# A spectral filter beside product-key experts: first transform by pairs of tiles, forward stage in four-byte 32x32 blocks, and a new order

## The chip, the cores and the metric

One core of a Trainium2 chip runs the whole program. The time is device microseconds of that core, from a run's first instruction to its last with what lies around them. Lower is better.

## The reference

`x` has 2048 rows of 576. It is normalised by rows, and two branches of the normalised `xn` are added to it.

```python
xn = _layernorm(x, axis=-1)
return x + _A_ref(xn, A_w_r, A_w_i) + _B_ref(xn, B_w_q, B_k1, B_k2, B_u, B_v)

# A: a filter in the frequency plane
X = rfft2(xn, axes=(-2, -1)) * (w_r + 1j * w_i)
y = irfft2(X, s=(S, D))

# B: for each of 32 heads the best of 8 + 8 keys picks one of 64 experts
q = einsum("nd,dhc->nhc", xn, w_q);  q1, q2 = q[..., :128], q[..., 128:]
i1, i2 = argmax(q1 @ k1.T), argmax(q2 @ k2.T);  e = i1 * 8 + i2
out = sum over heads of gelu(xn @ u[e]) * v[e]          # softmax over one entry is 1
```

## The kernel before

The 2048 rows lie as 16 tiles `t` of 128 rows (row 16 n + t is in partition n). `XN` holds all of `x`.

**Spectral branch.** The transform over the 2048 rows is split as 128 times 16. `folds(t)` uses the symmetry of cosine and sine: it adds and subtracts a tile's columns and their mirror image (`t1` buffers, then `A2` buffers), so that later transforms run over 145 and 144 columns. `dft128(t)` multiplies the folded tile by the 128-point matrix `Rs` (four-byte matmuls; `Rs` is the constant `Rm` times the row scale `rr`), and its result is split into two two-byte halves, `AB` (128 partitions) and `ABL` (the 33 columns left over). Row frequencies now lie in 16 groups `g`. `d_fwd(g)` transforms along the 576 columns (`c16` holds its two-byte constants, forward and inverse) and splits its result into two halves again: ScalarE copies it as the high half, VectorE subtracts for the low one. `s_fwd(g)` does the 16-point stage for groups g and g+1: 64x64 blocks with constants `s16`, three matmuls for each product (high by high, low by high, high by low). `s_mul(g)` multiplies by the filter `W`, scaled by its largest element (`w_scale`), `s_inv(g)` and `d_inv(t)` go back, and `fin(t)` does the inverse 128-point stage with `RT`, adds the experts' part and `x`, and stores.

**Expert branch.** Only differences of keys matter, so `fold_part(b, s)` multiplies `w_q` by them: 16 calls, each with two loads `w` of 576 KB and eight matmuls against `KP` (four-byte; four blocks of 128x32 side by side). `fold_scale`, `fold_end` and `fold_last` bring the result into `MU` and `MUL`. Then `x_t(r)` loads and scales the transposed `x`, `scores(r)` multiplies it by `MU`, and `route(r)` and `combine(r)` pick the experts and build `CAT` for `fin`. All scores wait for the last `fold_part`.

**Order.** Calls are not issued as written. `_Plan.add` records each operation; matmuls in a row of one stage are joined up to a planned cost of 900. `issue` then emits all operations in the order of a table of numbers, `RANK`; a string `PICK` says for the free choices which engine does it (`v` VectorE, `a` ScalarE, `g` GpSimd). `follow` walks the same order to place PSUM tiles in the eight banks. Each engine runs its instructions in that order. All loads and stores are issued by SyncE, whose queue is in order too: a load that waits for its buffer holds up those behind it. Every instruction is emitted in one line, L493, so the profile's rows are told apart by tiles: `banks` is PSUM, `A` an `A2` buffer, `s` the `s16` constants, `c` a constant (`c32` or `c16`), `t` a `t1` or `t2` buffer.

Of the kernel before, what the change touches and what calls it, by code (L numbers as in the profile page):

```python
# [32 lines left out]
def _consts():  # L33
# [40 lines left out]
    pair = np.arange(128).reshape(16, 2, 2, 2).transpose(2, 0, 1, 3).ravel()  # L74
    row = np.arange(128).reshape(16, 2, 2, 2).transpose(1, 0, 2, 3).ravel()
# [3 lines left out]
    def halves(m):  # L79
        return np.concatenate([m[:, :64, :64], m[:, 64:, 64:]], 1)  # L80

    def tr(m):
        m = m.transpose(0, 2, 1).reshape(16, 128, 16, 8).transpose(0, 1, 3, 2).reshape(16, 128, 128)
        return halves(m)
# [3 lines left out]
    U, V = halves(U[:, row]), halves(V[:, row])  # L88
    fw = np.concatenate([U, V, -U], 2)
    swap = np.arange(128) ^ 64  # L90
    kk[1::2], iv[1::2] = kk[1::2][:, swap], iv[1::2][:, swap]
    s16 = np.concatenate(_hl(fw * 64) + _hl(iv), 2)
# [7 lines left out]
    C1 = np.where((j <= 144)[:, None] == ev[None, :], C1, 0)  # L100
    S1 = np.sin(pi2 * (d1[:, None] * ll[None, :] % 576) / 576)
# [27 lines left out]
    c16 = np.concatenate([dc.reshape(128, -1), dl.reshape(128, -1),  # L129
                          ic.reshape(128, -1), il.reshape(128, -1)], 1)  # L130
    return c32, c16, s16, kk, ll


INF = float("inf")

# [1054 lines left out]
```

## Time and profile before

| | |
|---|---|
| median of 3 runs | 214.52 us (214.12 to 215.97) |
| the profiled execution | 214.62 us, span 212.8 us |
| TensorE clock granted | 0.998 |
| read from HBM, written | 38.33 MB, 4.72 MB |
| PE, DVE, POOL, ACT busy | 192.7, 195.5, 136.1, 129.8 us |

PE is TensorE, PEld its weight loads, DVE VectorE, ACT ScalarE, POOL GpSimd, SP SyncE. A row of the groups reads: line, engine, operation, output<-inputs, shape, count, then busy us and mean ns of one, then the idle time just before and who ended it. PE's busy time is modelled from pipelined matmuls; what a matmul costs is read from one start to the next.

### The profile page before, as it was taken

The page shows a single profiled execution, that of the slowest core. Times are in us where ns is not written, and L with a number is a line of the kernel's source. Part 1 is how long each engine was busy: PE and PEld are TensorE (multiplying, and loading weights), DVE is VectorE, ACT ScalarE, POOL GpSimd, SP SyncE. Part 2 cuts the span into 40 slices and gives each one's busy share as a digit, 9 for nine tenths or more (in the row PEclk, how much of TensorE's full clock was granted, in tenths as well). Part 3 has the DMA queues.
Part 4 walks back from the last instruction along what each step waited for, and adds up shares of the span by engine and source line. Part 5 has one row for each costly group of instructions (what it writes and reads, how often), then busy time and mean ns, then how long its engine had stood idle before and what let it go on. Part 6 is the DMA issues. An engine that isn't in the chain of part 4 may idle for free.

```text
span 212.8 us, 5984 instructions
## 1 busy us (share of the span) xinstructions
PE 192.7 (91%) x2287; PEld 134.7 (63%) x2287; DVE 195.5 (92%) x471; ACT 129.8 (61%) x280; POOL 136.1 (64%) x199
## 2 busy tenths in 40 slices
PE   0069998989998999999999999999999999999992
PEld 0067765677765775847465656665566887687871
DVE  0999999898799999997999999999999999999972
ACT  2278988788756973896958554757676453122430
POOL 2777789673339822885498244966696379549870
PEclk9999999999999999999999999999999999999999
DMA  5999999999999999308436012451100001071156
GB/s 159 398 414 425 408 401 395 370 366 403 372 313 353 391 269 373 102 34 338 147 104 223 10 40 64 137 184 32 38 0 5 0 5 55 0 273 63 55 204 243
DMA packets 14572, 43.43 MB, mean 204 GB/s; under 512 B 1872, under 2 KB 4688, under 8 KB 14160
## 3 DMA queue, kind: packets, MB, share of 16 engines
q1 hardware_dynamic: 14544, 43.05, 55.3%
q8 instruction: 18, 0.29, 0.6%
q14 instruction: 10, 0.08, 0.1%
HBM read 38.33 MB, written 4.72 MB: 202 GB/s over the span
## 4 chain that ended last, share of the span: by engine, by line
PE 44%; DVE 30%; DMA 8%; POOL 8%; issue 6%; ACT 1%; SPq 0%; POOLq 0%; DVEq 0%
PE banks L493 44%; DVE t L493 7%; DMA w<-in_wq_dram 6%; DVE w L493 5%; DVE A L493 5%; POOL A L493 4%; DVE MT L493 4%; DVE AB L493 3%; DMA XN<-in_x_dram 3%; POOL t L493 2%; DVE mx L493 2%; DVE st L493 2%; DVE XN L493 1%; DVE ABL L493 1%; POOL mv L493 1%
## 5 line engine op out<-in xcount | busy, mean ns | idle before, releaser
L493 PE MATMUL banks<-MU,xT 128*128 128x512 f16 x192 | 46.1, 380 | 0.0
L493 POOL TENSOR_TENSOR A<-t 128x287 f32<-128x287 f32 (+3 forms) x46 | 31.4, 698 | 10.5 <-DVE t L493 5.7
L493 PEld LDWEIGHTS <-xT 128*128 128x128 f16 x224 | 21.0, 98 | 22.7 <-DVE MU L493 0.2
L493 PE MATMUL banks<-c,AB 128*128 128x145 f16 (+1 forms) x384 | 34.4, 228 | 0.0
L493 PEld LDWEIGHTS <-AB 128*128 128x128 f16 x384 | 31.5, 122 | 1.7
L493 PE MATMUL banks<-Rs,A 128*128 128x128 f32 x128 | 19.8, 302 | 13.9 <-DVE Rs L493 12.6
L493 POOL TENSOR_TENSOR xT<-xf,xT 128x512 f16<-128x512 f32 (+1 forms) x28 | 24.1, 863 | 11.9 <-PE banks L493 5.5
L493 POOL TENSOR_TENSOR y<-t,t 128x289 f32<-128x289 f32 x30 | 20.8, 713 | 16.7 <-DVE t L493 16.1
L493 PEld LDWEIGHTS banks<-Rs,A 128*128 128x128 f32 x128 | 17.3, 209 | 17.2 <-DVE Rs L493 13.1
L493 POOL TENSOR_TENSOR yh<-y,yh 128x578 f16<-128x578 f32 x16 | 20.9, 1311 | 8.0 <-ACT yh L493 5.9
L493 DVE SCALAR_TENSOR_TENSOR t<-banks,wx,Wt 128x578 f32<-128x578 f32 x32 | 24.2, 812 | 0.4 <-PE banks L493 0.3
L493 PE MATMUL banks<-A,c 128*128 128x288 f32 x64 | 21.9, 424 | 0.4 <-DVE XN L493 0.4
L493 DVE TENSOR_TENSOR AB<-banks,AB 128x512 f16<-128x512 f32 x32 | 21.5, 676 | 0.3 <-ACT AB L493 0.3
L493 PE MATMUL banks<-w,KP 128*32 128x288 f32 x256 | 20.3, 415 | 1.1 <-DMA w<-in_wq_dram 0.9
L493 ACT ACTIVATE yh<-banks,sc 128x580 f32<-128x580 f32 x16 | 11.5, 744 | 15.8 <-PE banks L493 11.5
L493 ACT ACTIVATE AB<-banks 128x512 f16<-128x512 f32 x32 | 18.7, 591 | 3.1 <-PE banks L493 2.9
L493 PE MATMUL banks<-c,ABL 99*128 99x289 f16 (+1 forms) x64 | 18.5, 290 | 0.0
L493 ACT ACTIVATE ABL<-banks 99x256 f16<-99x256 f32 x32 | 12.0, 381 | 8.4 <-PE banks L493 7.8
L493 POOL TENSOR_TENSOR t<-yh 128x288 f32<-128x288 f32 x16 | 12.2, 765 | 6.6 <-ACT yh L493 4.1
L493 ACT ACTIVATE MT<-banks 128x256 f16<-128x256 f16 (+1 forms) x12 | 5.7, 472 | 16.5 <-PE banks L493 14.7
L493 POOL TENSOR_TENSOR t<-XN 128x289 f32<-128x289 f32 x17 | 13.1, 776 | 3.0 <-DMA XN<-in_x_dram 2.2
L493 DVE SCALAR_TENSOR_TENSOR XN<-banks,sc,XN 128x576 f32<-128x576 f32 (+1 forms) x18 | 13.1, 743 | 1.5 <-PE banks L493 1.4
(136 smaller groups left out, 438.2 us busy)
## 6 DMA issues: line engine op xcount, KB each, us to landing
w<-in_wq_dram SPq DMA_DIRECT2D x32, 576.0 KB, 6.8
xf<-in_xT_dram SPq DMA_DIRECT2D x16, 320.0 KB, 3.4
Wt<-in_W_dram SPq DMA_DIRECT2D x8, 578.0 KB, 5.1
out_dram<-XN SPq DMA_DIRECT2D x14, 288.0 KB, 3.2
XN<-in_x_dram SPq DMA_DIRECT2D x3, 1154.0 KB, 9.6
s<-in_s_dram SPq DMA_DIRECT2D x16, 192.0 KB, 4.1
XN<-in_x_dram SPq DMA_DIRECT2D x2, 577.0 KB, 5.0
c<-in_c_dram SPq DMA_DIRECT2D x1, 868.5 KB, 7.2
```

Source lines behind the costliest of these rows:

```text
L493: fn(*[x.place() if isinstance(x, _Ps) else x for x in args], **{k: x.place() if isinstance(x, _Ps) else x for k, x in kw.items()})
```

## The change

- **First transform.** `folds(t, n)` takes two tiles at once (the first two tiles are loaded, normalised and folded singly); `dft128(t)` takes a pair and three banks, and its evictions are twice as wide. The row mean is no longer subtracted: the column of the zero frequency is zero in the forward constants.
- **Forward stage.** `d_fwd` leaves its result in four bytes, one copy and no subtraction. `s_fwd(g, m)` does four groups and one of the two output parts, in 32x32 blocks of four bytes: 32 matmuls into four tiles of one bank. `s_mul(g, m)` multiplies one part by both parts of the filter; the splitting into halves moves to `s_inv`.
- **Constants.** `s16` becomes `fw` (four-byte, one load for four groups) and `iv` (two-byte, one load for two groups); `c16` becomes `cf` (forward) and `ci` (inverse), two loads.
- **Filter scale** for four groups at once, then four times; before one of four groups and six of two.
- **End.** `d_inv` takes two tiles; the factor `sc[12]` is multiplied into `RT` once.
- **Order, engines and buffers**: `RANK` and `PICK` are new; some buffers have another count (`xf` 2 for 3, `A2` 6 for 4).

```diff
+    def quarters(m):
+        return np.concatenate([m[:, 32 * a:32 * a + 32, 32 * a:32 * a + 32] for a in range(4)], 1)
...
+    C1[:, ll == 0] = 0
...
 RANK = (
-    3, 19, 14, 16, 76, 107, 2, 75, 51, 39, 143, 181, 0, 6, 15, 22, 13, 25, 1, 12, 40, 237, 5, 4, 8, 9, 7,
+    3, 9, 4, 8, 10, 11, 13, 2, 58, 18, 59, 67, 516, 5, 17, 7, 16, 15, 182, 25, 0, 1, 6, 20, 19, 34, 36, 23,
...
-    LOADS = ((0, 2), (2, 2), (4, 4), (8, 4), (12, 4))
+    LOADS = ((0, 1), (1, 1), (2, 2), (4, 4), (8, 4), (12, 4))
...
-    def folds(t):
-        xn = XN[:, t]
-        e = T([128, 2, L], F32, "eo", 2, "t1")
-        FG.tt(e[:, 1], xn[:, 0:289], xn[:, 576:287:-1], OP.subtract)
-        FG.tt(e[:, 0], xn[:, 0:289], xn[:, 576:287:-1], OP.add)
...
-        V.scalar_tensor_tensor(F[:, 0, 0:145], e[:, 0, 0:145], rr[:, 2, t:t + 1], e[:, 0, 288:143:-1],
-                               op0=OP.add, op1=OP.add)
+    def folds(t, n):
+        x = XN[:, t:t + n]
+        e = T([128, n, 2, L], F32, "eo", 4, "t1")
+        FV.tt(e[:, :, 0], x[:, :, 0:289], x[:, :, 576:287:-1], OP.add)
+        FG.tt(e[:, :, 1], x[:, :, 0:289], x[:, :, 576:287:-1], OP.subtract)
+        F = T([128, n, 2, L], F32, "F", 6, "A2")
+        FV.tt(F[:, :, :, 0:145], e[:, :, :, 0:145], e[:, :, :, 288:143:-1], OP.add)
+        FV.tt(F[:, :, :, 145:289], e[:, :, :, 143::-1], e[:, :, :, 145:289], OP.subtract)
...
+        p = PS("x", (128, 3, 512))
...
     def d_fwd(g):
...
-        t = T([128, 2, 2, L], F16, "A2", 2)
-        FP.copy(t[:, 0], p[:, :, :L])
-        V.tensor_tensor(t[:, 1], p[:, :, :L], t[:, 0], op=OP.subtract)
-        A2[g] = t
+        A2[g] = T([128, 2, L], F32, "A2", 6)
+        FP.copy(A2[g], p[:, :, :L])
...
-    def s_fwd(g):
-        ps = [PS("b"), PS("b")]
...
-                            P.matmul(ps[q][o:o + 64, m, :L], s[r, ha, 64 * w:64 * w + 64], A2[g + q][r, hb, b, :],
-                                     start=(n == 0), stop=(n == 5), tile_position=(64 * e, o))
+    def s_fwd(g, m):
+        ps = [PS("q", (128, 512)) for q in range(4)]
+        plan.pack, plan.cap = {p.tile for p in ps}, 1400
+        for b in range(2):
+            w = 32 * (0, 1, 1, 2)[2 * m + b]
+            for k in range(4):
+                r = slice(32 * k, 32 * k + 32)
+                for q in range(4):
+                    o = 32 * (k ^ q)
+                    P.matmul(ps[q][o:o + 32, :L], FW[g][r, q, w:w + 32], A2[g + q][r, b, :], start=(b == 0), stop=(b == 1),
+                             tile_position=(32 * k, o))
...
-    def s_mul(g):
+    def s_mul(g, m):
+        x, w, sw = PF.pop(g)[:, :L].unsqueeze(1).to_broadcast([128, 2, L]), Wt[g], wx[:, 1, g:g + 1]
+        if m == 0:
+            Y[g] = T([128, 2, L], F32, "y", 4)
+            V.scalar_tensor_tensor(Y[g], x, sw, w, op0=OP.mult, op1=OP.mult)
+            return
+        y, t = Y[g], T([128, 2, L], F32, "t1", 4)
+        V.scalar_tensor_tensor(t, x, sw, w, op0=OP.mult, op1=OP.mult)
+        FG.tt(y[:, 0], y[:, 0], t[:, 1], OP.subtract)
+        FG.tt(y[:, 1], y[:, 1], t[:, 0], OP.add)
...
-    for g in range(4):
-        load_s16(g)
+    load_fw(0)
     w_scale(0, 4)
...
+    for g in range(0, 16, 4):
+        for q in range(g, g + 4):
+            d_fwd(q)
+            if q % 2 == 0:
+                if q > 2:
+                    load_w(q)
+                load_iv(q)
...
+        for m in range(2):
+            s_fwd(g, m)
+            for q in range(4):
+                s_mul(g + q, m)
```

What the new order and the new loads do is shown at three places. The first is SyncE's queue in the middle of the `wq` loads (`w`): `c_72` is the whole `c16`, `s_0` and its like one group's `s16`, `xf` transposed `x`. Before:

```order
L493 DMA w_118<-in_wq_dram 128x1152
L493 DMA c_72<-in_c_dram 128x3474
L493 DMA xf_123<-in_xT_dram 128x640
L493 DMA Wt_113<-in_v_dram 128x576
L493 DMA w_119<-in_wq_dram 128x1152
L493 DMA s_0_114<-in_s_dram 128x768
L493 DMA w_120<-in_wq_dram 128x1152
L493 DMA s_1_115<-in_s_dram 128x768
L493 DMA w_122<-in_wq_dram 128x1152
```

and in the change, where buffers of one name are one tile (`cf`, `fw` and `iv` are the new constants):

```order
L491 DMA w<-in_wq_dram 128x1152 x2
L491 DMA cf<-in_cf_dram 128x1734
L491 DMA w<-in_wq_dram 128x1152 x2
L491 DMA xf<-in_xT_dram 128x640
L491 DMA w<-in_wq_dram 128x1152 x3
L491 DMA fw<-in_fw_dram 128x384
L491 DMA w<-in_wq_dram 128x1152 x2
L491 DMA iv<-in_iv_dram 128x768
```

`c16` is loaded by half, and one `fw` and one `iv` stand where `s16` loads for four groups began. The second place is the same queue at the last `wq` loads. Before, with the filter (`Wt`) for the fourth pair of groups behind:

```order
L493 DMA w_121<-in_wq_dram 128x1152
L493 DMA s_1_115<-in_s_dram 128x768
L493 DMA s_0_114<-in_s_dram 128x768
L493 DMA w_118<-in_wq_dram 128x1152
L493 DMA w_119<-in_wq_dram 128x1152
L493 DMA w_122<-in_wq_dram 128x1152
L493 DMA s_2_116<-in_s_dram 128x768
L493 DMA s_3_117<-in_s_dram 128x768
L493 DMA Wt_112<-in_W_dram 128x1156
```

and in the change:

```order
L491 DMA w<-in_wq_dram 128x1152 x5
L491 DMA Wt<-in_W_dram 128x1156
L491 DMA w<-in_wq_dram 128x1152 x3
L491 DMA Wt<-in_W_dram 128x1156
L491 DMA xf<-in_xT_dram 128x640
L491 DMA iv<-in_iv_dram 128x768
L491 DMA fw<-in_fw_dram 128x384
```

No constants stand among the last eight `wq` loads any more, but one filter load, for groups 4 and 5, does; `iv` and `fw` for later groups and `ci` (after these rows) come behind. The third place is PE where the first forward stage follows a fold. Before, weight loads and matmuls of two groups alternate:

```order
L493 LDWEIGHTS AB
L493 MATMUL banks<-c_72,AB 128x145
L493 MATMUL banks<-w_120,KP 32x288 x4
L493 LDWEIGHTS s_0_114
L493 MATMUL banks<-A_0_98,s_0_114 64x289
L493 LDWEIGHTS s_1_115
L493 MATMUL banks<-A_1_99,s_1_115 64x289
```

and in the change:

```order
L491 MATMUL banks<-w,KP 32x288 x8
L491 MATMUL banks<-A_95,fw 32x289 x32
L491 LDWEIGHTS ABL
L491 MATMUL banks<-cf,ABL 128x289
L491 LDWEIGHTS AB
```

Four-byte matmuls carry their weight loads with them, so the half stage is one row of 32, and `d_fwd` of a later group follows it; the second half stands behind `d_fwd` and two more fold groups. In all there are 64 matmuls of the forward stage, 126 of `d_fwd` and 66 of `s_inv` ahead of the last fold group in the change, against 144, 112 and 144 before.

More of the change, by code (lines that the diff above doesn't have):

```diff
@@ L390, in add @@
         if (eng == "tensor" and last is not None and last.eng == eng and last.stage == self.stage
-                and last.cost + c < 900 and (last.tiles == tiles or last.tiles | tiles <= self.pack)):
+                and last.cost + c < self.cap and (last.tiles == tiles or last.tiles | tiles <= self.pack)):
             op, i = last, len(self.ops) - 1
@@ new lines, in dft128 @@
+        p = PS("x", (128, 3, 512))
+        for i in range(2):
+            for c in range(4):
+                b, s = divmod(c, 2)
+                P.matmul(p[:, i, 128 * c:128 * c + 128], F[i][:, b, 161 * s:161 * s + 128], Rs[i], start=True, stop=True)
+        for i in range(2):
+            for b in range(2):
+                P.matmul(p[:99, 2, 256 * i + 128 * b:256 * i + 128 * b + 128], FL[i][:, b].rearrange("p a b -> p (a b)"),
+                         Rs[i], start=True, stop=True)
+        n = slice(2 * t, 2 * t + 4)
@@ L709, in dft128 @@
+        m = p[:, 0:2].rearrange("p i (h e) -> p h i e", e=2)
+        hi, ab = (AB[:, q].rearrange("p c (h n) -> p (c h) n", n=32)[:, :, n].rearrange("p h (i e) -> p h i e", e=2)
+                  for q in range(2))
         FP.copy(hi, m)
         V.tensor_tensor(ab, m, hi, op=OP.subtract)
-        lo = ABL[:99].rearrange("p b (h n) -> p (b h) n", n=64)[:, :, 4 * t:4 * t + 4]
+        l = p[:99, 2].rearrange("p (i h e) -> p h i e", i=2, e=2)
+        lo = ABL[:99].rearrange("p b (h n) -> p (b h) n", n=32)[:, :, n].rearrange("p h (i e) -> p h i e", e=2)
@@ new lines, in s_fwd @@
+    def s_fwd(g, m):
+        ps = [PS("q", (128, 512)) for q in range(4)]
+        plan.pack, plan.cap = {p.tile for p in ps}, 1400
+        for b in range(2):
+            w = 32 * (0, 1, 1, 2)[2 * m + b]
[5 more added lines that the diff above has]
+                             tile_position=(32 * k, o))
+        plan.pack, plan.cap = set(), 900
+        for q in range(4):
@@ L1003, in s_mul, with s_inv @@
+    @staged
+    def s_inv(g):
+        y = Y.pop(g)
         yh = T([128, 2, 2, L], F16, "yh", 2)
@@ L1076, in fin @@
             Q.dma_start(os[:, t, 288 * a:288 * b], x[:, 288 * a:288 * b])
-    for k, (t, n) in enumerate(LOADS):
+    for t, n in LOADS:
+        for i in range(t, t + n, 2):
+            folds(i, min(2, n))
         ln(t, n)
-        for i in range(t, t + n):
-            folds(i)
-            if i:
-                dft128(i - 1)
-    dft128(15)
+        for i in range(t & ~1, t + n & ~1, 2):
+            dft128(i)
     x_scale()
@@ L1114, in _body @@
     fold_last()
-    for r in range(3):
+    for r in range(2):
         x_t(r)
-    scores(0)
-    for g in range(4):
-        d_fwd(g)
-    s_fwd(0)
-    s_mul(0)
-    s_mul(1)
-    s_fwd(2)
-    for g in range(16):
-        s_inv(g)
-        if g + 2 < 16:
-            s_mul(g + 2)
-        if g + 4 < 16:
-            d_fwd(g + 4)
-            load_s16(g + 4)
-            if g % 2 == 1:
-                s_fwd(g + 3)
-        if g + 4 < 16 and g % 2 == 1:
-            load_w(g + 3)
-            w_scale(g + 3, 2)
-        r = g // 2
-        if g % 2 == 0:
-            if r < 5:
-                x_t(r + 3)
+    for g in range(0, 16, 4):
[5 more added lines that the diff above has]
+                load_iv(q)
+        if g:
+            w_scale(g, 4)
+        if g:
+            load_fw(g)
+        for m in range(2):
+            s_fwd(g, m)
+            for q in range(4):
+                s_mul(g + q, m)
+        for q in (g, g + 2):
+            s_inv(q)
+            s_inv(q + 1)
+            r = q // 2
+            scores(r)
+            if r < 6:
+                x_t(r + 2)
             route(r)
-        else:
-            if r < 7:
-                scores(r + 1)
             combine(r)
     w_end()
-    yq = {0: d_inv(0)}
-    for t in range(16):
-        if t + 1 < 16:
-            yq[t + 1] = d_inv(t + 1)
-        fin(t, yq.pop(t))
+    Q.dma_start(ci, a["ci"])
+    y = d_inv(0)
+    for t in range(0, 16, 2):
+        n = d_inv(t + 2) if t < 14 else None
+        for q in range(2):
+            fin(t + q, y[:, q])
+        y = n
 def _arrays(inp):
-    c32, c16, s16, kk, ll = _consts()
+    c32, cf, ci, fw, iv, kk, ll = _consts()
     g = lambda n: np.asarray(inp[n])
@@ L1173, in _arrays @@
         "c32": c32,
-        "c16": c16,
-        "s16": s16,
+        "cf": cf,
+        "ci": ci,
+        "fw": fw,
+        "iv": iv,
     }
```

253 lines of the change are left out of this document (111 added, 142 removed), and 123 rows, old and new, of the table RANK.

## Prediction

> **What bounds the kernel now.** I read the page's parts 1 and 2 first, then a table of busy time by stage, then the chain of waits.
>
> ```profile
> span 212.8 us, 5984 instructions
> ...
> PE 192.7 (91%) x2287; PEld 134.7 (63%) x2287; DVE 195.5 (92%) x471; ACT 129.8 (61%) x280; POOL 136.1 (64%) x199
> ...
> DMA  5999999999999999308436012451100001071156
> ```
>
> PE and DVE are both above 90%, and the DMA line reads nine tenths from 5 us to about 85 us and little afterwards. So the span has two parts with different limits. The table by stage (us of the stage, then busy us of each engine with its count, granted clock, DMA share, GB/s):
>
> ```profile
> core 0: us, PE busy (x) PEld busy (x) DVE busy (x) ACT busy (x) POOL busy (x), PEclk, DMA share, GB/s
> 12.60:50.00 37.40, 35.32 (x311) 26.98 (x312) 35.54 (x109) 31.45 (x87) 28.29 (x45) 1.00 1.01 396
> 50.00:84.00 34.00, 32.91 (x579) 23.23 (x578) 31.41 (x71) 23.48 (x48) 16.28 (x22) 1.00 0.99 355
> 84.00:130.00 46.00, 46.00 (x537) 28.15 (x537) 43.92 (x95) 32.84 (x61) 30.03 (x36) 1.00 0.37 123
> 130.00:170.00 40.00, 39.89 (x564) 26.07 (x553) 39.75 (x92) 26.18 (x57) 26.68 (x34) 1.00 0.19 59
> 170.00:209.00 39.00, 38.56 (x313) 30.23 (x311) 37.31 (x81) 12.20 (x22) 28.25 (x42) 1.00 0.28 105
> ```
>
> From 84 us on PE is busy 124.5 of 125 us, at full clock, while the DMA engines are at a third of their time. Before 84 us the DMA share is 1.0, and PE has lost 3.2 us of 71.4 since its first matmul. What ties the two parts together is the chain:
>
> ```profile
> 76.56 0.17 SPq L493
> 76.78 6.19 DMA w<-in_wq_dram
> 83.02 47.76 PE banks L493 x566
> ...
> 185.07 23.89 PE banks L493 x183
> 208.98 0.52 DVE XN L493
> ```
>
> The last load of `wq` lands at 83.0, the last fold matmuls follow (sixteen passes, about 1 us by the rows below), and then PE runs with hardly a gap to 185.07 + 23.89 = 209.0. So the span is made of three terms: the end of the last fold, **T**, at about 84.0; what PE has left after it, **R** = 209.0 - 84.0 = 125.0; and a tail of 212.8 - 209.0 = 3.8. The profiled execution took 214.62 us, so 1.8 us lie around the span; the median of the runs shown is 214.52.
>
> **T, the loads.** The two halves of the loaded part, and the loads of the page's part 6:
>
> ```profile
> 2.30:43.00 40.70, 29.09 (x255) 21.96 (x256) 35.58 (x121) 27.37 (x79) 30.09 (x54) 1.00 1.00 391
> 43.00:83.00 40.00, 38.17 (x620) 27.84 (x618) 37.41 (x85) 29.90 (x61) 20.54 (x28) 1.00 0.99 357
> w<-in_wq_dram SPq DMA_DIRECT2D x32, 576.0 KB, 6.8
> ...
> s<-in_s_dram SPq DMA_DIRECT2D x16, 192.0 KB, 4.1
> ...
> c<-in_c_dram SPq DMA_DIRECT2D x1, 868.5 KB, 7.2
> ```
>
> The stream never pauses, so T moves with the bytes that stand ahead of the last `wq` load on SP. Before, six `s16` loads (6 x 192 = 1152 KB) and the whole `c16` (868.5 KB) stand there. In the change one `fw` and one `iv` load (128 x 384 x 4 and 128 x 768 x 2 bytes, 192 KB each) and `cf` alone (128 x 1734 x 2 bytes, 433.5 KB) stand there; `ci` comes later. As many `wq`, `W` and `xT` loads are ahead as before. That is 1203 KB less, 1.23 MB, at 357 GB/s **3.4 us**; at the first half's 391 it is 3.2. I take T = 80.6.
>
> Can PE follow? Its busy time ahead of 84 us was 35.3 + 32.9 = 68.2 us. The rows of the timeline (start, length, engine, group) give the pieces that change sides; the distance between starts is what a piece costs PE:
>
> ```profile
> 58.38 1.68 PE L493 MATMUL banks<-A,s 64*64 64x289 f16 x48
> 59.98 1.18 PE L493 MATMUL banks<-w,KP 128*32 128x288 f32 x16
> 61.09 0.30 PE L493 MATMUL banks<-c,ABL 99*128 99x289 f16 x1
> 61.23 0.55 PE L493 MATMUL banks<-c,AB 128*128 128x145 f16 x6
> ...
> 62.12 0.29 PE L493 MATMUL banks<-c,ABL 99*128 99x289 f16 x1
> ...
> 67.38 0.69 PE L493 MATMUL banks<-w,KP 128*32 128x288 f32 x8 [0.73 <-DMA w<-in_wq_dram]
> 68.00 0.30 PE L493 MATMUL banks<-c,ABL 99*128 99x289 f16 x1
> ...
> 70.14 0.84 PE L493 MATMUL banks<-s,yh 64*128 64x128 f16 x24
> ...
> 71.16 0.83 PE L493 MATMUL banks<-s,yh 64*128 64x128 f16 x24
> ...
> 74.18 0.38 PE L493 MATMUL banks<-c,mxr 128*128 128x1 f32 x2
> 74.43 1.29 PE L493 MATMUL banks<-c,MT 128*128 128x128 f32 x9
> ```
>
> One old forward stage of two groups costs 1.60 us, one `d_fwd` 1.03, one `s_inv` 1.02. Ahead of the last fold the change has one `d_fwd` more, two half stages (priced below at 1.11) in place of three stages of 1.60, and 66 in place of 144 inverse matmuls (36 are an `s_inv`, so -2.2): 68.2 + 1.0 - 2.6 - 2.2 = 64.4. With the old start at 12.6 PE could be there at 77.0, ahead of the loads at 80.6. The loads decide.
>
> **The forward stage.** In four bytes a matmul is two passes: the fold rows show it (256 records for 128 matmuls). Sixteen fold passes took 1.11 us (59.98 to 61.09) and eight 0.62 (67.38 to 68.00), so a set of four side by side takes 0.245 and the change of shape 0.13. A half stage of four groups is 32 matmuls, 64 passes. Sixteen blocks of 32x32 at once make four sets of it, 4 x 0.245 + 0.13 = **1.11 us**; four at once, as in the fold, would be sixteen sets, 4.05 us. No row shows sixteen; both ends stay in the range. I take 1.11, since the old stage fills its array: 48 matmuls of 289 columns in 1.60 us are 0.133 for four, and one `c,ABL` matmul of 289 columns also costs 0.13 (61.09 to 61.23). All eight: 8 x 1.60 = 12.8 becomes 8.9.
>
> [...] In the change the four row tiles of each of the four outputs write one bank. [...]
>
> **R, after the last fold.** The change leaves six half stages where there were five stages: 6 x 1.11 - 5 x 1.60 = -1.3. One `d_fwd` less, -1.0. 510 inverse matmuls for 432, +2.2. The filter scale by four groups leaves three reductions there for five, about 0.25 and 0.1 each by the `mxr` row (74.18 to 74.43): -0.7; three transposes more of two passes, +0.9 by the `MT` row (nine passes in 1.29). Scores, `d_inv` and `fin` keep their matmuls. The sum is 0.1; I keep R = 125.0 and bound it by the waits below.
>
> **What lies beside other work.** These rows carry the engines' edits:
>
> ```profile
> L493 DVE SCALAR_TENSOR_TENSOR t<-banks,wx,Wt 128x578 f32<-128x578 f32 x32 | 24.2, 812 | 0.4 <-PE banks L493 0.3
> L493 DVE TENSOR_TENSOR A<-banks,A 128x578 f16<-128x578 f32 x16 | 12.0, 749 | 0.7 <-ACT A L493 0.7
> L493 POOL TENSOR_TENSOR t<-XN 128x289 f32<-128x289 f32 x17 | 13.1, 776 | 3.0 <-DMA XN<-in_x_dram 2.2
> L493 DVE SCALAR_TENSOR_TENSOR A<-t,rr 128x145 f32<-128x145 f32 x16 | 6.7, 431 | 0.7 <-POOL rr L493 0.4 <-POOL t L493 0.3
> L493 DVE TENSOR_TENSOR t<-XN 128x289 f32<-128x289 f32 x15 | 6.6, 443 | 0.0
> PE banks L493 <- DVE Rs L493: 12.6, 1, 12.6
> ```
>
> DVE loses 16 subtractions of `d_fwd` (12.0 us) and 16 folds with the mean (6.7); its 32 products by the filter stay. In R it loses 7 x 0.75 = 5 us of 121. Since PE was busy 124.5 of 125 there, I count nothing for it. Folds by pairs are 578 columns; that form isn't shown, so it lies between one and two of the 289 rows, 0.78 to 1.55 us on POOL and 0.44 to 0.89 on DVE; I take the upper end. All of this lies under the loads: the first transform ended near 50 us, 30 us before T, and an engine that gains there hands it to the loads. The single first tiles may start PE up to 1 us before 12.6; that too ends at the loads. The scale moved from `d_inv` into `RT`, constants cut out of `mk`, and fewer scale reductions cost nothing: they shorten engines that wait in R. If the cover goes, a late fold of a pair costs 0.7 us each.
>
> A new wait stands on SP: the third `W` load is ahead of the last three `wq` loads, and its buffer is freed by the products of groups 0 and 1, second half. Queued behind it are those three loads, and the last folds and all of R wait for them. By the order PE does that half ahead of four `d_fwd`, nearly two `s_inv` and eight fold groups, 12 us of its own time before the last fold; four products of 0.81 us and four loads of 576 KB at 357 GB/s (1.65 each) take 9.8 of it. It just fits, so I count nothing; each microsecond by which it doesn't is one on T.
>
> **Sum.** 80.6 + 125.0 + 3.8 = 209.4 of span, 211.2 with the 1.8. The chance that the products and the freed DVE close part of the gaps in R (PE lost 0.5 us of 125 by busy time, though switches of shape hide in that) is worth half a microsecond: **210.8 us**, 1.7% under the median. One per cent, 2.1 us, is about what a measurement of this kernel tells from no change.
>
> **Rivals.**
> *The loads run faster* (chance 0.17). The second half's 357 GB/s is below the first's 391 with the DMA share at 1.0. If fewer loads of 1.5 KB rows bring 391, then 14.3 - 1.2 = 13.1 MB take 33.5 us from 43: the last `wq` lands at 76.5, T = 77.5, which PE can just follow (77.0): 208.1, and 206 with a second microsecond out of R. Against it: the rate also fell while only `w` was loading.
> *The banks run out* (0.18). A half stage fills four banks, and each is freed only by a product of 0.81 us: 3.2 us for four, against 1.11 on PE. Groups 4 to 7 run both halves in a row, all eight banks, with `d_fwd` right behind. Waiting for two products and their start is about 2 us there, less in the three other groups, where scores stand between: 3 to 4 us in R, **214 to 215**, no change. For it: PE waits for nobody in R now. Against: four banks per stage were needed before too.
> *The blocks of one bank take turns* (0.08). The slower side: four at a time, 4.05 us a half stage, six in R: 6 x 2.94 = +17.6, **228 us**. It decides from where a half stage takes over 2.1 us (break-even with 1% slower, 216.7), that is from seven blocks at once downwards. Against: the 0.133 for four above.
> *The change doesn't cut the stream* (0.05): a wait on SP for a buffer (`xf` has two now, not three) stops the loads as long as the bytes save: 214.5.
>
> **How the numbers follow.** The forecast has 0.52, from 208.5 to 213. The range of 8 in 10 takes in the faster loads and the banks and leaves out the slow blocks: 205.5 to 215.5. Faster by over 1% (under 212.4): seven eighths of 0.52, and 0.17, 0.63 with rounding. Within 1%: the rest of 0.52, most of the banks' 0.18 and half of the last: 0.24. Slower: 0.13.
>
> **What would show it.** The last `wq` landing near 79.6 with DMA share 1.0 up to it; the last fold's end near 80.6; a half stage at 1.1 us from start to start; PE busy within a microsecond of the whole from there to 4.1 us before the end. It is wrong if PE idles after T, if the DMA line has holes before T, or if PE reaches the last fold only after its load has long landed.

## The result, and the profile after

The changed kernel is **slower**: 221.0 us in the median of four runs (220.47 to 221.86), against 214.32 (213.65 to 215.97) of the kernel before beside it. The ratio is 1.030, with an interval of 1.024 to 1.037. The forecast was 210.8. The profiled execution took 220.77 us, 1.8 of them around the span as before, so it stands 9.6 us above the forecast's own sum for such an execution (211.2). Parts 1 and 2 of the page of the changed kernel:

```profile
span 219.0 us, 6067 instructions
...
PE 191.9 (88%) x2406; PEld 130.3 (60%) x2406; DVE 181.0 (83%) x404; ACT 127.9 (58%) x268; POOL 141.6 (65%) x178
...
PEclk9999988999999999999999999999999999999999
DMA  5999999899999995756223340240202020102276
```

PE is busy as long as before (191.9 for 192.7 us), DVE 14.5 us less, and the span is 6.2 us longer. Two things are new: the clock line has two eights, and the DMA line dips to eight tenths in the eighth slice (38 to 44 us). The table by stage (the columns as in the prediction, PEclk third from last) puts them into one stage:

```profile
14.10:50.00 35.90, 31.72 (x284) 24.44 (x285) 30.57 (x69) 27.20 (x68) 26.46 (x25) 0.95 0.96 349
50.00:84.00 34.00, 32.49 (x520) 21.70 (x521) 20.57 (x47) 23.37 (x44) 16.24 (x21) 1.00 0.99 370
84.00:130.00 46.00, 44.52 (x750) 28.68 (x749) 39.01 (x81) 36.82 (x73) 31.69 (x38) 1.00 0.44 136
130.00:170.00 40.00, 39.94 (x535) 23.92 (x533) 38.95 (x90) 23.84 (x50) 27.82 (x34) 1.00 0.17 51
170.00:215.00 45.00, 43.23 (x325) 31.60 (x323) 42.56 (x90) 13.90 (x30) 30.18 (x44) 1.00 0.24 92
```

In the first stage PE idles 4.2 us where it idled 2.1, at a clock of 0.95 and 349 GB/s for 396. In the second it idles 1.5 us for 1.1, and part 5 of the two pages says what the folds' matmuls wait for, before and after:

```profile
L493 PE MATMUL banks<-w,KP 128*32 128x288 f32 x256 | 20.3, 415 | 1.1 <-DMA w<-in_wq_dram 0.9
```

```profile
L491 PE MATMUL banks<-w,KP 128*32 128x288 f32 x256 | 21.2, 431 | 1.5 <-DMA w<-in_wq_dram 1.5
```

The chain of waits, in order of time (start, length, what):

```profile
10.60 1.16 DVE rr L491
11.78 1.23 DVE rr L491
14.15 4.44 PE banks L491 x24
...
28.41 2.51 DVE rr L491 x2
31.05 8.23 PE banks L491 x63
...
49.88 27.27 PE banks L491 x413
77.16 6.05 DMA w<-in_wq_dram
83.25 0.74 PE banks L491 x8
...
206.91 7.92 PE banks L491 x44
```

By the prediction's three terms: T, the end of the last fold, is 83.25 + 0.74 = 84.0, as before and not the forecast 80.6. R is 206.91 + 7.92 - 84.0 = 130.8, not 125.0. The tail is 219.0 - 214.8 = 4.2 for 3.8. So of the 9.6 us, 3.4 are in T, 5.8 in R and 0.4 in the tail. T adds up on PE: its busy time from the first matmul to T fell from 68.2 to 64.2 us (forecast 64.4; up to 1.7 of the 64.2 is half clock, below), but it started 1.6 us later and idled 5.7 us for 3.2 (1.5 of the 5.7 for the last two `wq` loads).

New on the chain are the tiles `rr`, the statistics of a few columns. DVE's row on the timeline around the first and the second place (start, length, operation, shape):

```profile
10.14 0.33 DVE L491 SCALAR_TENSOR_TENSOR rr<-mv,rr 128x1 f32<-128x1 f32 x1
10.52 1.22 DVE L491 SCALAR_TENSOR_TENSOR rr<-mv,rr 128x1 f32<-128x1 f32 x1
11.78 1.23 DVE L491 SCALAR_TENSOR_TENSOR rr<-rr 128x1 f32<-128x1 f32 x1
13.05 0.10 DVE L491 SCALAR_TENSOR_TENSOR rr<-rr 128x1 f32<-128x1 f32 x1
...
28.41 1.25 DVE L491 TENSOR_TENSOR rr<-rr,mv 128x16 f32<-128x16 f32 x1 [0.17 <-ACT y L491]
29.59 1.33 DVE L491 SCALAR_TENSOR_TENSOR rr<-mv,rr 128x4 f32<-128x4 f32 x1
```

and POOL's and PE's at the same times:

```profile
10.41 2.58 POOL L491 TENSOR_TENSOR t<-XN 128x578 f32<-128x578 f32 x2
...
28.32 2.57 POOL L491 TENSOR_TENSOR t<-XN 128x578 f32<-128x578 f32 x2
...
27.80 1.15 PE L491 MATMUL banks<-w,KP 128*32 128x288 f32 x16
31.05 0.37 PE L491 MATMUL banks<-c,bx 128*1 128x128 f32 x1 [2.10 <-DVE bx L491]
31.35 2.15 PE L491 MATMUL banks<-w,KP 128*32 128x288 f32 x16
```

One and the same operation on one column takes 0.10 us at 13.05 and 1.23 us at 11.78. The long ones end when one of POOL's folds of a pair ends (two of 1.29 us from 10.41, so at 11.7 and 13.0; two from 28.32, at 29.6 and 30.9). At the first place this delays PE's start to 14.15 (12.59 before). At the second PE waits 2.10 us for `bx`, and then sixteen fold passes take 2.15 us for 1.15: the clock is halved for 3.41 us (31.02 to 34.44), which costs up to 1.7 us.

### The profile page after: what moved, and what is told of

It is laid out like the page before. It is cut to its first block, busy times and chain, and to the rows that moved or that the text cites. A ratio compares the mean times of both kernels' runs of the same rounds, so it can differ in the third digit from the quotient of the medians.

```text
span 219.0 us, 6067 instructions
## 1 busy us (share of the span) xinstructions
PE 191.9 (88%) x2406; PEld 130.3 (60%) x2406; DVE 181.0 (83%) x404; ACT 127.9 (58%) x268; POOL 141.6 (65%) x178
## 3 DMA queue, kind: packets, MB, share of 16 engines
HBM read 37.54 MB, written 4.72 MB: 193 GB/s over the span
## 4 chain that ended last, share of the span: by engine, by line
PE 45%; DVE 27%; ACT 12%; DMA 5%; POOL 5%; issue 3%; SPq 1%; DVEq 0%; ACTq 0%
PE banks L491 45%; DVE w L491 5%; DVE MT L491 5%; DVE XN L491 3%; DVE AB L491 3%; DMA w<-in_wq_dram 3%; ACT t L491 3%; DVE rr L491 3%; DMA XN<-in_x_dram 3%; POOL y L491 2%; DVE t L491 2%; ACT y L491 2%; DVE ABL L491 2%; ACT AB L491 2%; POOL A L491 1%
## 5 line engine op out<-in xcount | busy, mean ns | idle before, releaser
L491 POOL TENSOR_TENSOR A<-t 128x289 f32<-128x289 f32 (+5 forms) x39 | 36.7, 962 | 15.0 <-DVE t L491 10.3
L491 PE MATMUL banks<-act,A 128*128 128x128 f32 x128 | 18.7, 303 | 16.2 <-ACT act L491 14.2
L491 POOL TENSOR_TENSOR y<-y,t 128x289 f32<-128x289 f32 x32 | 24.2, 781 | 10.0 <-DVE y L491 7.5
L491 PEld LDWEIGHTS banks<-act,A 128*128 128x128 f32 x128 | 17.0, 213 | 20.0 <-issue 16.0
L491 DVE TENSOR_TENSOR AB<-banks,AB 128x512 f16<-128x512 f32 (+1 forms) x24 | 20.1, 855 | 4.4 <-ACT AB L491 3.5
L491 ACT ACTIVATE AB<-banks 128x512 f16<-128x512 f32 (+1 forms) x24 | 17.5, 738 | 3.9 <-PE banks L491 1.9
L491 PE MATMUL banks<-cf,AB 128*128 128x144 f16 (+1 forms) x192 | 17.4, 227 | 0.3 <-issue 0.3
L491 PE MATMUL banks<-ci,AB 128*128 128x145 f16 x192 | 17.2, 228 | 0.0
L491 ACT ACTIVATE xf<-xf,bx 128x640 f32<-128x640 f32 x16 | 13.3, 829 | 4.3 <-DMA xf<-in_xT_dram 4.2
L491 DVE TENSOR_TENSOR w<-w,MT 128x512 bf16<-128x512 bf16 (+1 forms) x24 | 13.7, 581 | 0.1
```

The source lines that it names most:

```text
L491: fn(*[x.place() if isinstance(x, _Ps) else x for x in args], **{k: x.place() if isinstance(x, _Ps) else x for k, x in kw.items()})
```

## The experiments

Ratios are against runs of the kernel before beside them (medians 214.8 to 215.1 us). A time without a range is a single run. Of the last two kernels only the traces are read, since the one run of the kernel before beside them took 218.0 us.

**Do the loads set T in the kernel before?** No change of order, only more bytes: the constants `c16` are loaded twice, then three times, ahead of the last `wq` load.

```diff
-    Q.dma_start(c16, a["c16"])
+    for i in range(2):          # the second kernel: range(3)
+        Q.dma_start(c16, a["c16"])
```

> The kernel before, with its constants c16 loaded twice, 868.5 KB more ahead of the last wq loads, issued at 31 us. If the stream of loads sets its last fold, as the prediction has it, the last fold ends 2.3 to 2.5 us later, at 86.4 us, and the time is 216.8 us. If the stream is held by buffers that come free late, it is under 1 us later, at most 215.5 us.

> The kernel before with its constants c16 loaded three times, 1737 KB more ahead of the last wq loads, issued at about 20, 30 and 41 us. If the stream of loads sets its last fold: 4.6 to 5 us later, 219 us. If TensorE's work does (theory E, as the single additional load has it) and the stream has room: under 1.5 us, at most 215.5 us.

Measured: 213.72 and 216.47 us. The last fold's last matmul starts at 82.82 with 868 KB more and at 83.59 with 1737 KB more, where it starts at 83.79 without. The stage from 50 to 67 us, of the kernel before and of the one with `c16` twice:

```profile
50.00:67.00 17.00, 16.64 (x266) 11.87 (x265) 14.75 (x33) 11.71 (x23) 8.03 (x11) 1.00 0.99 353
```

```profile
50.00:67.00 17.00, 16.71 (x269) 11.46 (x269) 15.31 (x33) 11.09 (x22) 8.77 (x12) 1.00 1.03 403
```

A DMA share of 0.99 at 353 GB/s becomes 1.03 at 403 GB/s: in this kernel a share of 1.0 did not mean that the DMA engines could do no more. By the 357 GB/s of the prediction 1737 KB would have cost 5.0 us; they cost nothing on T. (The 2.7 us by which that run is longer than with `c16` twice lie behind T for the most part: 127.0 us from the last fold's to the last of all matmuls, for 125.1.) In the chain of waits of the kernel with `c16` twice no load of `wq` stands at all; TensorE and the products do (with `c16` three times loads stand on it up to 67.8 us, and T still has not moved):

```profile
45.70 18.73 PE banks L495 x273
65.01 2.99 DVE t L495 x4
...
72.31 8.29 PE banks L495 x150
81.53 3.00 DVE t L495 x4
...
86.53 43.49 PE banks L495 x511
```

So the bytes of the stream did not set T. What bytes taken off it could still have saved is bounded by the 0.9 us that the folds' matmuls wait for `wq` in the kernel before.

**More bytes in the changed kernel.** `cf` loaded three times.

```diff
-    Q.dma_start(cf, a["cf"])
+    for i in range(3):
+        Q.dma_start(cf, a["cf"])
```

> The changed kernel with the forward constants cf loaded three times instead of once, 888 KB more among the wq loads, issued between 28 and 35 us. If the stream of loads sets the last fold (the prediction's step for T), it ends 888 KB / 357 to 391 GB/s = 2.3 to 2.5 us later, at 86.4 us, and the time is 223.4 us. If the stream has holes that TensorE makes by freeing the buffers of wq late (theory A), the additional loads fall partly into the holes after 35 us: 0 to 1.2 us later, 221 to 222.2 us.

Measured: 222.12 us, the last fold's last matmul at 83.95 (83.53 without). The last `wq` load lands at 83.41 for 83.20, so the stream has room here too. But it took 7.2 us from its issue for 6.05 (issued at 76.20 and 77.16, each behind a fold that freed its buffer), and PE, 0.9 us earlier at the fold before (79.59 for 80.51), stood 2.2 us for it (1.1 without the bytes). So in the changed kernel the last load is a second, nearly equal bound on T.

**Are POOL's wide folds what T lost?** The fold of a pair stays one step of the order, but POOL gets it as two instructions of a single tile each, not one of double width.

```diff
-        FG.tt(e[:, :, 1], x[:, :, 0:289], x[:, :, 576:287:-1], OP.subtract)
+        # what falls to POOL, here and in F's two parts:
+        for i in range(2):
+            FG.tt(e[:, i, 1], x[:, i, 0:289], x[:, i, 576:287:-1], OP.subtract)
```

> The changed kernel, in which each fold of a pair that POOL does is issued as two instructions of one tile each; the work is the same. Theory P (a DVE instruction with two inputs in SBUF waits for the POOL instruction that runs beside it, so that wide POOL instructions hold small ones of DVE longer): the four instructions on rr that took 1.22 to 1.33 us take at most 0.75, the first matmul starts about 1 us earlier (13.2 us instead of 14.15), the wait for bx shrinks from 2.1 to about 1 us, and the time falls by 1 to 2.5 us, to 218.5 to 220. Rival Q (these instructions are long for another reason, or POOL's fixed cost of some 60 ns for 26 more instructions eats it): they stay at 1.2 us, 221 us or 0.5 more.

Measured: 216.52 us (216.36 to 218.05), ratio 1.011 (1.005 to 1.016). DVE's and PE's rows:

```profile
10.51 0.34 DVE L491 SCALAR_TENSOR_TENSOR rr<-mv,rr 128x1 f32<-128x1 f32 x1
10.89 0.71 DVE L491 SCALAR_TENSOR_TENSOR rr<-mv,rr 128x1 f32<-128x1 f32 x1
11.64 0.62 DVE L491 SCALAR_TENSOR_TENSOR rr<-rr 128x1 f32<-128x1 f32 x1
...
29.20 0.27 PE L491 MATMUL banks<-c,bx 128*1 128x128 f32 x1 [0.61 <-DVE bx L491]
29.41 1.18 PE L491 MATMUL banks<-w,KP 128*32 128x288 f32 x16
...
79.12 0.69 PE L491 MATMUL banks<-w,KP 128*32 128x288 f32 x8
```

The stalls shrink with POOL's instruction, from 1.2 us to 0.7. By the changed kernel's rows two folds of one tile (0.69 us) are 0.07 us longer than one of a pair (1.31); measured, POOL's 18 more instructions add 2.4 us to its busy time (144.0 for 141.6), 0.13 each. PE starts at 13.40, waits 0.61 us for `bx` by this row, and the clock stays full (sixteen passes in 1.18 us). The last fold ends at 79.75, where the next matmul starts, and nothing stands in its row that PE waited for. The last `wq` load lands 4.8 us after its issue, for 6.05. The stage table shows 50 to 80 us at a DMA share of 1.00 with PE busy 29.68 of 30.10. R is 130.7 us by the starts of the last fold's and of all last matmuls (131.0 in the changed kernel): of the 4.3 us between the two profiled executions, 4.1 are in T (79.41 for 83.53). The shorter stalls, the full clock and the end of the 1.5 us of waiting for `wq` all come with the one edit; no run parts them.

**Later, not shorter.** The transposition of `bx` is put five pairs later in PE's order, where it waits for nobody.

```diff
+RANK = list(RANK)
+for _i, _r in {236: 194.2, 237: 194.4, 238: 194.6, 239: 194.8, 240: 194.9}.items():
+    RANK[_i] = _r
```

> The changed kernel, in which TensorE asks for the maximum of x (the small transposition behind DVE's bx) only after the fifth pair of the first transform instead of ahead of it. Theory A (the loads starve because TensorE stands still): TensorE no longer idles 2.1 us at 29 us and keeps its full clock (3.4 us at half clock cost it 1.7), so the folds free the buffers of wq some 3 us earlier, the last fold ends at 81 to 82 us instead of 84.0, and the time falls from 221.0 to 218 to 219 us. Rival B (the stream of loads sets the last fold whatever TensorE does before 50 us): the last fold stays at 84 us, 221 us. Rival C (behind the idle time the next pair's folds on POOL are late as well): the idle time moves, at most 1 us is won.

Measured: 219.43 us (217.89 to 221.24), ratio 1.019 (1.011 to 1.027); no half clock, the last fold's last matmul at 82.32. The stalls of 1.1 to 1.3 us stay, and PE idles at another wait: 1.35 us before 34.99, for ACT's `yl`. The gain is a third of what the split brings. Both edits together:

> Both edits at once: POOL's folds of a pair issued tile by tile, and TensorE asking for the maximum of x only after the fifth pair. If what is left of TensorE's standing still (1.0 us ahead of the small transposition in the kernel with single folds) still delays the last fold, the last fold ends near 79.2 us instead of 80.1 and the time is 215 to 216 us instead of 216.5. Rival: the loads or the next folds set the last fold by now, and the time stays at 216.5 or grows as the pair behind it comes later.

Measured: 218.1 us (215.99 to 218.7, ten runs), ratio 1.013 (1.010 to 1.017); two of the ten took 216.0 and the other eight 217.6 to 218.7. The trace is of one of the two; in it the last fold's last matmul starts at 80.23. So the second edit brings nothing beyond the split alone.

**Shorter still.** POOL's folds in quarters.

```diff
-            FG.tt(e[:, i, 1], x[:, i, 0:289], x[:, i, 576:287:-1], OP.subtract)
+            for c in (slice(0, 145), slice(145, 289)):
+                ...  # the same subtraction, columns c
```

> As with single folds, but each of POOL's folds of a pair in four instructions of about 145 columns. If DVE waits for the POOL instruction beside it, the small instructions on rr that took up to 0.8 us with single folds take at most about 0.5; the first matmul starts a further 0.3 to 0.6 us earlier. POOL pays about 60 ns more for each of some 36 instructions, 2 us, of which the first transform feels a part. Time 215.5 to 217 us. If their length doesn't come from POOL's, they stay near 0.7 to 0.8 us and POOL's cost alone is seen: 217 to 218 us.

Measured: 222.59 us (222.24 to 224.9), ratio 1.039 (1.031 to 1.046), which neither theory had. POOL's 36 more instructions add 5.7 us to its busy time (149.7 for 144.0). The timeline, DVE and POOL:

```profile
30.15 2.51 POOL L491 TENSOR_TENSOR t<-XN 128x145 f32<-128x145 f32 x6
...
30.85 5.25 DVE L491 SCALAR_TENSOR_TENSOR rr<-rr 128x4 f32<-128x4 f32 x2
...
32.68 3.41 POOL L491 TENSOR_TENSOR A<-t 128x144 f32<-128x144 f32 x8
...
36.35 0.38 PE L491 MATMUL banks<-c,mxr 128*128 128x1 f32 x2 [3.90 <-DVE mxr L491]
```

Most stalls are now 0.49 us or less, but two small instructions of DVE (1.84 and 3.50 us) end only when a whole run of POOL's instructions is through: the rest of one and four more, then eight. PE waits 3.9 us and gets another period of half clock. Pieces alone don't help, then. But a gapless row on POOL is not enough to keep DVE out either: at 11.3 to 12.6 us of the same trace three such instructions of DVE take 0.36 to 0.41 us, each ending with one of POOL's quarters, which follow each other without a gap there too, and in the changed kernel DVE got its turn between two wide folds (11.74 in the rows above). What decides is not shown.

**DVE takes the first folds.** On top of the split, the two folds of tiles 2 and 3 that POOL did beside DVE's first small instructions go to DVE and stand earlier.

```diff
+PICK = PICK[:18] + "vv" + PICK[20:]
+# and RANK[59] = 56.2, RANK[60] = 56.4
```

> Single folds, and the two folds of tiles 2 and 3 that POOL did from 10.4 to 13.2 us, beside DVE's small instructions on rr for the first tiles, are done by DVE behind those instructions. If DVE waits for the POOL instruction beside it, the four instructions on rr between 10.9 and 13.7 us, 2.6 us together, fall to about 0.15 us each, and the first matmul starts at 12.0 to 12.6 us instead of 13.4; of this some 0.5 to 1 us reaches the end (DVE has 1.5 us more to do there): 215.5 to 216 us for 216.5. If they are long for another reason, nothing moves, or DVE's additional work makes it 217.

Measured: 216.38 us (214.63 to 218.08, ten runs), ratio 1.007 (1.003 to 1.011), the nearest of these versions to the kernel before. PE starts at 12.08 as expected, but idles 0.7 and 1.5 us before 17.97 and 23.03 and 1.5 us for `wq` loads (none with the split alone), and the last fold's last matmul stands at 79.74 (79.41 with the split alone): the earlier start is handed back.

**What is the half stage's price?** It took 1.54 us from start to start for the forecast 1.11 (two in a row 2.96). First the banks: row block k writes bank k, and not all four rows of one output the same bank.

```diff
-                    P.matmul(ps[q][o:o + 32, :L], ...
+                    P.matmul(ps[k][o:o + 32, :L], ...
```

> The changed kernel, in which each of the four row blocks of the forward stage writes a bank of its own (bank k for row block k, where the change puts the four row blocks of a group into one bank); the four groups' results then come out in each other's places, so the filter and all behind it work on exchanged data. Theory S (a set of sixteen is held by the 32 instructions that start it, 16.7 ns a weight load and matmul, and by its late last block): a half stage stays at 1.60 us and the time at 221. Rival T (row blocks that write one bank hold each other up): the half stage falls to about 1.1 us, eight of them 4 us, and the time to 217 to 218.

Then, on top of the split, the order of the sixteen blocks: output by output, not row by row.

```diff
-            for k in range(4):
-                for q in range(4):
+            for q in range(4):
+                for k in range(4):
```

> Single folds, and in the forward stage the four row blocks take turns (the loops over groups and row blocks exchanged, the same 32 matmuls). If a set of sixteen is held by starting 32 instructions at 16.7 ns, the order doesn't matter: 1.54 us a half stage, 216.5 us. If neighbours in one row block hold each other up, the half stage falls towards 1.1 us and the time to about 213 us.

Measured: 221.76 and 216.89 us. The first half stage on PE's row, in the changed kernel, with a bank for each row block, and with the other order:

```profile
62.73 1.61 PE L491 MATMUL banks<-A,fw 32*32 32x289 f32 x64
```

```profile
62.94 1.60 PE L491 MATMUL banks<-A,fw 32*32 32x289 f32 x64
```

```profile
61.36 1.60 PE L491 MATMUL banks<-A,fw 32*32 32x289 f32 x64
```

Neither the banks nor this order matters. Then half the columns in each of twice as many matmuls, on top of the split:

```diff
-        for b in range(2):
+        for b, cs in [(b, slice(c, d)) for c, d in ((0, 145), (145, 289)) for b in range(2)]:
-                    P.matmul(ps[q][o:o + 32, :L], FW[g][r, q, w:w + 32], A2[g + q][r, b, :], ...
+                    P.matmul(ps[q][o:o + 32, cs], FW[g][r, q, w:w + 32], A2[g + q][r, b, cs], ...
 # and plan.cap = 4000, so that they stay in one row
```

> Single folds, and every matmul of the forward stage in two of 145 and 144 columns: the same products from twice as many weight loads and matmuls. If a set of sixteen blocks is held by starting its 32 instructions (16 times 16.7 ns = 0.27 us, where the columns need 0.245 for 289 and 0.12 for 145), a half stage takes 8 times 0.27 and 0.4, 2.5 us, and the time is 223 to 224 us. If the streaming of the columns holds it, a half stage stays near 1.6 us and the time at 217.

Measured: 231.38 us; a half stage alone takes 1.95 us, between the two theories, so neither the columns nor the count of passes sets it alone. (The time itself says little of the stage: PE also stands still for 3.35 and 3.45 us with no releaser in the trace, and the clock is halved for 10.2 us in all.) In the changed kernel's trace the 1st, 17th, 33rd and 49th of a half stage's 64 passes start 0, 0.27, 0.51 and 0.94 us after the first, and the matmul behind the stage after 1.54. In the first half the passes of a set start 7 ns apart and a set takes 0.27 and 0.24 us, as the forecast had it (0.245). In the second half they start 16 to 17 ns apart, and the two sets take 0.43 and 0.60 us, of which 0.13 is the change of shape by the prediction's estimate from the fold rows. So the expectations' 16.7 ns holds for the second half alone, and the 0.4 us too much lie there. Why the second half is slower stays open.

**Would a cheaper half stage have paid?** On top of the split, the second of the two matmuls of each output is left out.

```diff
-        for b in range(2):
+        for b in range(1):
         # and every matmul with start=True, stop=True
```

> Single folds, and the forward stage multiplies only one of its two input parts (16 of 32 matmuls a half stage; the other half of its products is left out), so a half stage falls from 1.54 to about 0.8 us. Theory E (TensorE's own work sets the last fold as well as the end): the last fold comes 1.5 to 2 us earlier and the time falls by 8 times 0.72, 5.5 to 6 us, to 211 us. Rival L (the loads set the last fold): it stays at 80 us, only the half stages behind it count, 212.5 us or more. Rival O (another engine sets the pace behind the last fold): under 2 us less, 215 us.

Measured: 218.41 us. The last fold's last matmul starts at 80.58, no earlier than with the split (79.41), though two lighter half stages lie ahead of it: PE starts 0.7 us later and waits 1.9 us for `wq` loads (none with the split). A half stage alone takes 0.7 us for 1.54, yet R is 131.4, not less than 130.7. PE waits instead (0.83 for ACT's `A`, 0.82 and 0.91 for DVE), and a period of half clock at 105.4 to 108.9 costs 1.7 us. So in R something paces PE nearly as tightly as its own work. DVE, busy 118 of 130 us there, is the candidate: lighter products by the filter, first with all forward matmuls, then with half of them.

```diff
+        c = slice(0, 145)
-        V.scalar_tensor_tensor(t, x, sw, w, op0=OP.mult, op1=OP.mult)
+        V.scalar_tensor_tensor(t[:, :, c], x[:, :, c], sw, w[:, :, c], op0=OP.mult, op1=OP.mult)
         # and POOL's two combinations behind it, columns c
```

> The version with single POOL folds; the second product by the filter of every group, and POOL's two combinations behind it, do 145 of 289 columns (the rest of their columns keep the first product alone, so those columns are another computation). VectorE loses about 0.38 us in each of 16 products, twelve of them behind the last fold: 4.6 us there. Theory P (behind the last fold TensorE's own matmuls decide): the last fold at 80.1 and the last matmul at 210 as without the edit, 130 us between them, at most half a microsecond less. Rival D (VectorE decides there): 125 to 126 us between them.

> The same edit on the kernel that multiplies one of the two parts of each input, half of the forward stage's matmuls left out. Alone, that left-out half moved the stretch behind the last fold from 130 to 131.5 us (1.7 of it a period of half clock). Theory O (TensorE and VectorE set the pace together, so that only both lighter are faster): 125 to 127 us from the last fold to the last matmul. Rival L (neither's sum decides, but the way from bank to product to bank, each with its start): 129 to 131 us.

Measured: 218.22 and 215.66 us. The window from 84 to 214 us: the split alone, with half the forward matmuls, with lighter products, with both:

```profile
84.00:214.00 130.00, 124.50 (x1563) 81.98 (x1545) 117.97 (x251) 71.40 (x145) 90.12 (x114) 1.00 0.29 96
```

```profile
84.00:214.00 130.00, 123.56 (x1387) 79.76 (x1386) 120.13 (x254) 71.31 (x145) 89.56 (x114) 0.99 0.30 98
```

```profile
84.00:214.00 130.00, 125.28 (x1583) 83.04 (x1583) 115.61 (x257) 72.23 (x147) 82.36 (x114) 1.00 0.30 99
```

```profile
84.00:214.00 130.00, 122.34 (x1390) 79.71 (x1390) 115.48 (x256) 71.92 (x146) 82.07 (x114) 0.99 0.30 100
```

R is 130.7, 131.4, 130.4 and 128.2 us in this order. DVE's relief (busy 115.8 us in R for 119.7) brings 0.3 alone; TensorE's alone nothing; both together 2.5. In both kernels with TensorE's relief a period of half clock costs about 1.7 (without it R would be about 129.7 and 126.5). These are single runs. The 128.2 lies between the two expected ranges: that the two engines set R's pace together is supported, not shown. The half clock lies at the same place in both kernels with half the matmuls (105.4 to 108.9 and 105.3 to 108.7 us), beside a wait of PE for DVE behind a half stage (0.82 and 1.51 us); with both edits:

```profile
103.05 1.35 PE L491 MATMUL banks<-A,fw 32*32 32x289 f32 x32 [0.50 <-ACT A L491]
105.92 4.12 PE L491 MATMUL banks<-MU,xT 128*128 128x512 f16 x12 [1.51 <-DVE ABL L491]
```

where twelve such matmuls take 2.76 us at full clock.

## Why the prediction was wrong

**"The loads decide T": the step that failed first.** It rested on the DMA share of 1.0 and the last load on the chain. Both extra loads in the kernel before left T where it was or earlier, so the bytes of the stream were no bound, and the 3.4 us for 1203 KB had no ground. The load on the chain was late because a buffer of `wq` was freed late: it is issued at 77.16, as the fold matmuls that end there free its buffer. "PE could be there at 77.0" was the term to go by: with the later start (1.6) and PE's idle time (5.7) it makes 84.3, for 84.0 measured. The loads keep a smaller part: PE's waits for `wq` are 0.9 us before, 1.5 in the change, nothing with the split and up to 2.7 in the other versions of the change.

**"All of this lies under the loads": the second.** With the stream as cover gone, the engines that feed the first transform count in full. The price of a pair's fold on POOL lay within its bounds (1.3 us, 0.78 to 1.55), but who stands behind it was not asked: DVE's small instructions with two inputs. They delay PE's start (0.75 us of the 1.6 come back with the split) and cost it 2.1 us at `bx` and up to 1.7 us of half clock. The traces have them at 1.22 to 1.33 us beside folds of 1.3 us, at 0.5 to 0.8 beside single ones (0.75 us in the mean) and at 0.10 with no fold beside them. So the wide folds carry a price that the prediction put at nothing.

That the split's T (79.75) comes near the forecast 80.6 is a coincidence. It comes from PE's work and not from the loads: from its first matmul to the last fold's last PE took 66.0 us with the split (13.40 to 79.41) and 71.2 before (12.59 to 83.79), since work ahead of the last fold was taken out or left for R, as the prediction itself counted.

**The half stage: mis-sized.** 1.54 us, not 1.11; all of the forward stage takes 12.8 us of PE as before (12.89, then 12.82), not 8.9. (The prediction says that both ends of this price stay in its range; the slow end, 228 us, lies outside it.) That four row blocks write one bank is not what costs it: with a bank for each the time is the same 1.54, and the 4.05 us of the slow end did not occur.

**R, "the sum is 0.1": +5.8.** From start to start, from 84 us on: the half stages make 9.75 us for 8.06 (forecast -1.3, so 3.0 off). `s_inv` makes 15.87 for 12.91, about half a microsecond of it the wait of the half stage behind it (forecast +2.2). `d_fwd` makes 7.81 for 8.35 (forecast -1.0). `d_inv`, expected to be unchanged, 0.7 more, with one wait of 0.9 for DVE. The reductions of the scale save 0.2 and not 0.7; the transpositions cost 1.2 (forecast 0.9). PE's idle time in R grows from 0.5 to 3.1 us: there were rivals for that. *The banks run out* named the groups right but not the size: two half stages in a row do not wait (2.96 for two). The gaps lie where a half stage waits for ACT's `A` (0.49 at 106.03, and 0.6 more inside that stage, 2.17 for 1.54) and where `d_inv` and `fin` wait for DVE (0.91 before 191.46, 0.53 before 206.91). "I count nothing" for DVE's relief was right: 4 us less for DVE behind the last fold (the kernel with lighter products) moved R by 0.3 us.

**The other rivals.** *Blocks take turns* fell with 1.54 (its bound was 2.1). *The loads run faster* came true in the kernel with more bytes (403 GB/s) and was worth nothing. *The change doesn't cut the stream*: it does (37.54 MB read in all for 38.33), and the time doesn't hang on it. The **new wait** on SP, the third `W` load, held nothing up: the last `wq` load was issued at 77.16 behind a buffer, 76.78 before.

Versions measured: the split at 216.5 and the split with DVE's first folds at 216.4 are the best, and neither beats the kernel before.

## What to carry to other kernels

A DMA line of nines was no limit here (353 GB/s at a share of 0.99 became 403 with more to load): before a time is built on a stream, load something twice in the kernel at hand and see whether the end moves. Before an instruction on POOL is made wider, list the short two-input instructions of DVE that run beside it (here 1.22 to 1.33 us for 0.10 to 0.18) and who waits for them; shorter pieces on POOL helped here at half the width and not at a quarter, so measure each. And where two engines are both above 90% of a stretch, do not count on the relief of one: here it was worth 0.3 us at most, and both together 2.5, which supports that they pace it together and does not show it.

## What the runs showed of the hardware

DVE's small two-input instruction took 0.10 us alone (one column), 1.23 beside a POOL fold of 1.3 us, and 3.50 (four columns) where POOL had eight short instructions in a row; beside another such row, three of them took 0.36 to 0.41.

TensorE's granted clock was 0.50 for 3.41 us at a time behind some short idle times and stayed at 1.00 behind others. It was halved after 2.1 us before 31.05 in the changed kernel (31.02 to 34.44), and after two waits of 0.8 us around 104 us with half the forward matmuls (105.4 to 108.9), but not after 1.35 us before 34.99 with `bx` later, nor after 1.5 before 23.03 with DVE's first folds. The same wait of 1.83 us for `bx` is followed by a halved clock with a bank for each row block, and not with `cf` three times. In the three traces with two periods apart (a bank for each row block, half columns, both reliefs) their starts lie 54.61, 23.89 and 27.31 us apart, 16, 7 and 8 times the 3.41 us of one period. What decides whether an idle time is followed by a halved clock is not shown.

Sixteen blocks of 32x32 ran side by side in the changed kernel: a set of sixteen passes of 289 columns, started 7 ns apart, takes 0.27 and 0.24 us in the first half of a half stage, about as long as four passes of a 128x32 fold (0.245). In the second half they start 16 to 17 ns apart and take about 0.4 us more in all, which no run here explains.
